# Hash attention with a maxout FFN on one Trainium2 core: who writes the hash rows, casts V and normalises

## The chip, the cores and the metric

The kernel runs on one core of a Trainium2 chip. The metric is device time in microseconds (us) of one launch, the median of three runs. PE is TensorE, DVE is VectorE, ACT is ScalarE, POOL is GpSimd, and SP is SyncE, which here only issues DMAs.

## What is computed

Attention over 4 batches, 8 heads, 768 positions, 64 dimensions per head, with a mask from a random-projection hash, followed by a feed-forward layer with a maximum of three products:

```
q_bits = (q @ proj > 0)              # 6 bits for each position
k_bits = (k @ proj > 0)
mask   = q_bucket == k_bucket        # the 6 bits read as a number
scores = where(mask, q @ k.T / 8, -1e9)
x      = softmax(scores) @ v         # then (batch*seq, heads*dim) = (3072, 512)
h      = max(x @ w1, x @ w2, x @ w3) # 512 -> 768
out    = h @ w_out                   # 768 -> 512
```

## The kernel before, in words

**Operands.** Heads go in pairs (b, pr): four pairs for each of four batches. For q and k of a pair, `split_h` (lines 139 to 146) makes a float16 high part and `split_r` (148 to 153, always DVE) the float16 remainder; both lie side by side in one tile, 128 values for a position. They are transposed into `T` (dimension by position): in batches 0 and 1 by PE (`pe_T`) with a DVE copy back (`evac_T`), in batches 2 and 3 by a transposing DMA on the SP queue (`xbar`, line 156). After the transpose the rows 0 to 63 of `T` hold the high part, the others the remainder.

**Hash rows.** `hash_mm` (172) projects `T` on PE, `hash_cmp` (183) turns the signs into +0.5 or -0.5 on DVE, and the six bits, scaled, are written into rows 64 to 69 of `T`. A score is then one matmul over 70 rows: keys of the same bucket get a fixed large bonus, which the exponential takes off again, so that others vanish. For the very first pair `hash_head` (208) writes these rows with DVE, one head at a time. For all other pairs, `hash_pair` (192) does both heads at once and scales the bits in place, and `hash_rows` (199) copies them with eight small DMAs of 4.5 KB on the SP queue (line 205).

**Units.** The work is 192 score units: a unit is two matmuls (`score`, line 244) into a PSUM tile and one exponential of 128x768 on ACT (line 253). Six units make a block, which is one half of the queries of one pair. `attend` (258) follows two units behind (LAG is 2) and accumulates into `av`, a PSUM pool with one buffer. When a block is complete, `norm` (278) adds a small term from the mean of V, takes the reciprocal (both DVE) and multiplies (POOL, line 290, but DVE for the last pair of a batch). `x_T` transposes the result on PE, with a DVE copy. `vcast` (218) casts V to float16 on POOL.

**FFN.** When a batch's half is complete, 18 first-layer atoms (four matmuls each, then an ACT copy for w1 and a DVE maximum for w2 and w3, lines 319 and 321) and three second-layer atoms (six matmuls, line 326) are put in a list. All share `mm_ps`, a PSUM pool with three buffers, with the transposes and hash products.

**Order.** The order is written out by hand: the loop over steps u (446) issues `score(u)`, `attend(u-2)`, then what `at(u, ...)` has listed, then FFN atoms as a credit allows, then what `at_end(u, ...)` has listed. Credit begins at step 41 and grows each step by `rate`, which spreads the FFN over the steps that are left. Each engine, and the SP queue, works through its own instructions in this order. `front` (387) prepares the pairs of batches 0 and 1 over some steps, `prep` (423) those of batches 2 and 3, and `tail` (402) places the hash. The hash of pair 0 of batch 2 comes at step 64, then at steps 75, 86, 97, 112, 123, 134 and 145. The loads of a pair (`load_pair`) stand eight steps ahead of its splits in the same SP queue; the first loads of batch 1 stand at step 25, behind the hash rows of batch 0 at steps 6, 15 and 22.

Of the kernel before, what the change touches and what calls it, by code (L numbers as in the profile page):

```python
# [10 lines left out]
FP16 = mybir.dt.float16  # L11
AluOp = mybir.AluOpType
# [4 lines left out]
def kernel(  # L17
# [12 lines left out]
    nc = tc.nc  # L30
    B, H, S, D = q.shape
    NBITS = proj.shape[1]
    P = 128
    NCH = S // P
# [4 lines left out]
    NP = H // 2  # L39
    HQ = S // 2  # L40
    CH = NCH // 2
# [14 lines left out]
    small = ctx.enter_context(tc.tile_pool(name="small", bufs=4))  # L56
    xp = ctx.enter_context(tc.tile_pool(name="xp", bufs=3))
    hp = ctx.enter_context(tc.tile_pool(name="hp", bufs=12))
    op = ctx.enter_context(tc.tile_pool(name="op", bufs=4))
# [38 lines left out]
    vones = []  # L98
    for i in range(2):
        t = konst.tile([P, H, NCH, D + 2], FP16, name=f"vone{i}", tag=f"vone{i}")  # L100
# [11 lines left out]
    def make_p(i):  # L112

        if i == 0:
            nc.vector.tensor_copy(ph[:], p32[:])
            nc.vector.tensor_tensor(out=pr32[:], in0=p32[:], in1=ph[:], op=AluOp.subtract)
        for o in (0, D):
            for l, src in ((PA, ph), (PB, pr32)):
                nc.vector.tensor_scalar(out=l[i][o : o + D, NBITS * i : NBITS * (i + 1)], in0=src[:],
                                        scalar1=1024.0, scalar2=None, op0=AluOp.mult)  # L120
# [10 lines left out]
    T = {}  # L131
# [7 lines left out]
    def split_h(n, b, pr, eng, heads=(0, 2)):  # L139
        a = slice(heads[0] * NCH, heads[1] * NCH)  # L140
        x32 = raws[n, b, pr][:].rearrange("p h (c d) -> p (h c) d", d=D)[:, a, :]
        o = S16[n, b, pr][:, a, 0:D]
        if eng is nc.scalar:
            nc.scalar.activation(o, x32, ActFn.Copy, scale=QS)  # L144
        else:
            eng.tensor_scalar(out=o, in0=x32, scalar1=QS, scalar2=None, op0=AluOp.mult)

    def split_r(n, b, pr, heads=(0, 2)):
        a = slice(heads[0] * NCH, heads[1] * NCH)
        x32 = raws[n, b, pr][:].rearrange("p h (c d) -> p (h c) d", d=D)[:, a, :]  # L150
        s = S16[n, b, pr]
        nc.vector.scalar_tensor_tensor(out=s[:, a, D : 2 * D], in0=x32, scalar=QS,  # L152
                                       in1=s[:, a, 0:D], op0=AluOp.mult, op1=AluOp.subtract)

    def xbar(n, b, pr):
        nc.sync.dma_start_transpose(T[n, b, pr][:], S16[n, b, pr][:].rearrange("p a d -> p (a d)"))
# [15 lines left out]
    def hash_mm(sets):  # L172

        hps = mm_ps.tile([P, 512], FP32, tag="mm", name="hps")
        ws = [(i, l[i]) for l in (PA, PB) for i in range(len(sets))]
        for m, (i, w) in enumerate(ws):
            for g, (t, hh, half) in enumerate(sets[i]):
                a = hh * NCH + half * CH
                nc.tensor.matmul(hps[32 * g : 32 * (g + 1), 0:HQ], w[:], t[:, a : a + CH, :],  # L179
                                 start=m == 0, stop=m == len(ws) - 1)  # L180
        return hps

    def hash_cmp(out, hps):
        nc.vector.tensor_scalar(out=out, in0=hps[:, 0:HQ], scalar1=0.0, scalar2=0.5,  # L184
                                op0=AluOp.is_gt, op1=AluOp.subtract)

    def hash_row(dst, src):
        nc.vector.tensor_scalar(out=dst, in0=src, scalar1=2 * BIT, scalar2=None, op0=AluOp.mult)

    hbs = {}  # L190

    def hash_pair(b, pr):
        hb = small.tile([P, HQ], FP16, tag="hb", name="hb")
        hbs[b, pr] = hb
        g = [(T[n, b, pr], hh) for hh in range(2) for n in "qk"]
        hash_cmp(hb[:], hash_mm([[(t, hh, half) for t, hh in g] for half in range(2)]))
        hash_row(hb[:], hb[:])

    def hash_rows(b, pr):
        hb = hbs.pop((b, pr))  # L200
        for g, (n, hh) in enumerate((("q", 0), ("k", 0), ("q", 1), ("k", 1))):
            for half in range(2):
                a = hh * NCH + half * CH
                o = 32 * g + NBITS * half
                nc.sync.dma_start(T[n, b, pr][D : D + NBITS, a : a + CH, :].rearrange("p a t -> p (a t)"),
                                  hb[o : o + NBITS, :])

    def hash_head(b, pr, hh):

        tq, tk = T["q", b, pr], T["k", b, pr]  # L210
        hb = small.tile([P, HQ], FP16, tag="hb", name="hb")
        hash_cmp(hb[:], hash_mm([[(tk, hh, 0), (tq, hh, 0), (tk, hh, 1), (tq, hh, 1)]]))
        for g, (t, half) in enumerate(((tk, 0), (tq, 0), (tk, 1), (tq, 1))):
            a = hh * NCH + half * CH
            hash_row(t[D : D + NBITS, a : a + CH, :].rearrange("p a t -> p (a t)"),
                     hb[32 * g : 32 * g + NBITS, :])

    def vcast(b, pr):
        v32 = raws.pop(("v", b, pr))[:].rearrange("p h (c d) -> p h c d", d=D)
        nc.gpsimd.tensor_copy(vones[b % 2][:, 2 * pr : 2 * pr + 2, :, 0:D], v32)  # L220

    mvs = {}

# [54 lines left out]
    def norm(b, hf, pr):  # L278
        av = avs.pop((b, hf, pr))[:, 0 : 2 * CH * W].rearrange("p (h c w) -> p h c w", h=2, c=CH)
        xn = xp.tile([P, CH, P], FP16, tag="xn", name="xn")  # L280
        xns[b, hf, pr] = xn
        xv = xn[:].rearrange("p c (h d) -> p h c d", h=2)
        rr = small.tile([P, 2, CH, 1], FP32, tag="rr", name="rr")
        t = small.tile([P, 2, CH, W], FP32, tag="t", name="t")
        nc.vector.tensor_tensor(out=t[:, :, :, 0 : D + 1], in0=av[:, :, :, 0 : D + 1],  # L285
                                in1=mvs[b, pr][:].unsqueeze(2).to_broadcast([P, 2, CH, D + 1]),
                                op=AluOp.add)
        nc.vector.reciprocal(rr[:], t[:, :, :, D : D + 1])  # L288
        eng = nc.vector if pr == NP - 1 else nc.gpsimd
        eng.tensor_tensor(out=xv, in0=t[:, :, :, 0:D], in1=rr[:].to_broadcast([P, 2, CH, D]),  # L290
                          op=AluOp.mult)

    def x_T(b, hf, pr):
        if (b, hf) not in xTs:
# [51 lines left out]
    todo = {}  # L346
    todo_end = {}

    def at(step, fn, pe=0.0):
        todo.setdefault(step, []).append((pe, fn))  # L350

    def at_end(step, fn):
        todo_end.setdefault(step, []).append(fn)
# [13 lines left out]
    split_h("k", 0, 0, nc.scalar, (1, 2))  # L367
    split_r("q", 0, 0, (1, 2))
    hash_head(0, 0, 0)
    make_p(1)  # L370
    vcast(0, 0)

    def first_b():
        split_r("k", 0, 0, (1, 2))
        pq = pe_T("q", 0, 0, 1)
        pk = pe_T("k", 0, 0, 1)
        evac_T(pq, "q", 0, 0, 1, nc.vector)
        evac_T(pk, "k", 0, 0, 1, nc.vector)

    at(0, first_b)  # L380
    at(1, lambda: hash_head(0, 0, 1))

    def load_pair(b, pr, eng):
        for n in "qkv":
            load(n, b, pr, eng)

    def front(b, pr, s):

        at(s, lambda: operands(b, pr))
        at_end(s, lambda: split_h("q", b, pr, nc.vector))  # L390
        at_end(s, lambda: split_h("k", b, pr, nc.vector if b == 0 else nc.scalar))
        at_end(s, lambda: split_r("q", b, pr))
        at_end(s + 1, lambda: split_r("k", b, pr))

        def tr(n, hh):
            evac_T(pe_T(n, b, pr, hh), n, b, pr, hh, nc.vector)

        for i, (n, hh) in enumerate((("q", 0), ("q", 1), ("k", 0), ("k", 1))):
            at(s + 2 + i // (2 if b == 0 else 1), lambda n=n, hh=hh: tr(n, hh), 0.34)
        tail(b, pr, s + (4 if b == 0 else 7))  # L400

    def tail(b, pr, s):
        at(s, lambda: hash_pair(b, pr), 0.67)
        at(s, lambda: hash_rows(b, pr))

    at(0, lambda: vcast(0, 1))
    at(0, lambda: load_pair(0, 2, nc.sync))
    front(0, 1, 2)
    at(2, lambda: meanv(0, 0), 0.34)
    at(3, lambda: load_pair(0, 3, nc.sync))  # L410
# [12 lines left out]
    def prep(b, pr, s):  # L423
        at(s, lambda: operands(b, pr))
        at_end(s, lambda: split_h("q", b, pr, nc.vector))
        at_end(s + 1, lambda: split_h("k", b, pr, nc.scalar))
        at_end(s + 1, lambda: split_r("q", b, pr))
        at_end(s + 1, lambda: xbar("q", b, pr))
        at_end(s + 3, lambda: split_r("k", b, pr))
        at_end(s + 3, lambda: xbar("k", b, pr))  # L430
        tail(b, pr, s + 12)

    for b in range(1, B):
        for pr in range(NP):
            s = 33 + 7 * pr if b == 1 else 2 * (b - 1) * NUG + 4 + 11 * pr
# [4 lines left out]

    N = len(units)
    begin = 6 * NUP + 5
    rate = (7 * 24 * 0.64 + sum(c for st, l in todo.items() if begin <= st < N for c, _ in l)
            + 0.2 * 28) / (N - begin)
    credit = 0.0
    for u in range(N + LAG + 4):
# [51 lines left out]
```

The softmax here doesn't subtract the row's maximum and nothing guards it: scores larger than these inputs give would overflow.

## Time and profile before

Median 319.71 us of three runs (318.12 to 321.54). The profiled execution spans 314.9 us.

| engine | busy us | share | instructions |
|---|---|---|---|
| PE | 279.7 | 89% | 2896 |
| ACT | 202.7 | 64% | 265 |
| DVE | 178.7 | 57% | 375 |
| POOL | 41.3 | 13% | 53 |

Where PE is not busy, by stretches of the timeline:

| us | steps | PE busy of it | granted PE clock |
|---|---|---|---|
| 24 to 32 | 8 to 13 | 4.11 of 8 | 0.89 |
| 32 to 40 | 13 to 18 | 7.81 of 8 | 0.68 |
| 56 to 64 | 35 to 41 | 6.14 of 8 | 1.00 |
| 72 to 80 | 47 to 51 | 6.38 of 8 | 1.00 |
| 88 to 96 | 56 to 59 | 5.47 of 8 | 0.79 |
| 120 to 128 | 75 to 77 | 4.82 of 8 | 0.65 |
| 192 to 200 | 122 to 126 | 6.03 of 8 | 1.00 |
| 208 to 216 | 132 to 136 | 5.71 of 8 | 1.00 |
| 288 to 296 | 189 to end | 5.77 of 8 | 1.00 |

A busy PE is not a PE at its peak: at a granted clock of half speed the same matmuls take longer and count as busy. The profile's chain of waits is followed back from the last instruction; a wait for several things is put down to the one that came last. "issue" is time in which an engine waited for nothing that the profile shows.

### The profile page before, as it was taken

What the parts mean: (1) busy time and instruction counts of PE and PEld (TensorE: products, weight loads), DVE (VectorE), ACT (ScalarE), POOL (GpSimd) and SP (SyncE); (2) the same over time, 40 slices, a digit from 0 to 9 for tenths busy, and PEclk for the clock granted to TensorE, in tenths of its full rate; (3) what the DMA queues carried; (4) which work ended last, traced back from release to release, by engine and by line L of the source; (5) the groups of instructions that cost most, each with busy time, mean ns of one, the idle gap of its engine ahead of it and who ended that gap; (6) DMA issues with size and microseconds to landing.
All of it is one profiled execution on the core that took longest, in us unless ns stands there. A gap on an engine that the chain in (4) does not pass through costs nothing.

```text
span 314.9 us, 7282 instructions
## 1 busy us (share of the span) xinstructions
PE 279.7 (89%) x2896; PEld 180.2 (57%) x2896; DVE 178.7 (57%) x375; ACT 202.7 (64%) x265; POOL 41.3 (13%) x53
## 2 busy tenths in 40 slices
PE   2895998798969994999999997979999999999794
PEld 1463765565647562565666664636666665665451
DVE  5766582797876652556476564736463454443552
ACT  3346479877736773676777776675767777777220
POOL 0304512120041101101102121120101110111000
PEclk9999699999989997799999999999999999999999
DMA  7905993918136058190938427092802002001002
GB/s 202 371 30 72 143 180 84 352 46 285 41 52 186 10 89 266 31 227 6 235 122 217 136 55 205 14 271 76 104 4 103 2 1 98 5 3 67 35 0 100
DMA packets 47138, 35.63 MB, mean 113 GB/s; under 512 B 27184, under 2 KB 44032, under 8 KB 47104
## 3 DMA queue, kind: packets, MB, share of 16 engines
q1 hardware_dynamic: 43072, 32.02, 36.7%
q0 software_dynamic: 3952, 3.15, 7.0%
q8 instruction: 22, 0.36, 0.4%
q14 instruction: 12, 0.10, 0.1%
q10 hardware_dynamic: 80, 0.00, 0.0%
HBM read 25.17 MB, written 6.29 MB: 100 GB/s over the span
## 4 chain that ended last, share of the span: by engine, by line
PE 74%; DMA 12%; DVE 8%; ACT 3%; issue 2%; SPq 0%; ACTq 0%; DVEq 0%
PE ps L314 27%; PE sc L249 17%; PE po L326 9%; PE av L269 9%; DMA kT<-ks 7%; PE hps L179 5%; PE tps L162 4%; ACT AT L253 3%; DMA k<-in_k_dram 2%; PE xps L300 2%; DVE ks L152 2%; DMA kT<-hb 1%; PE svp L228 1%; DMA q<-in_q_dram 1%; DVE hb L184 1%
## 5 line engine op out<-in xcount | busy, mean ns | idle before, releaser
L253 ACT ACTIVATE AT<-sc,bias_t 128x768 f16<-128x768 f32 x192 | 169.7, 901 | 73.4 <-PE sc L249 72.5
L314 PE MATMUL ps<-xT,w_sb 128*128 128x384 f16 x576 | 112.8, 330 | 4.2 <-DVE mv L231 4.2
L249 PE MATMUL sc<-qT,kT 70*128 70x384 f16 x384 | 98.6, 339 | 7.0 <-DMA kT<-hb 3.3
L269 PEld LDWEIGHTS <-AT 128*128 128x128 f16 x1152 | 62.4, 99 | 28.9 <-issue 4.6
L321 DVE TENSOR_TENSOR ht<-ht,ps 128x384 f16<-128x384 f16 x96 | 52.9, 551 | 45.3 <-PE ps L314 40.8
L269 PE MATMUL av<-vone,AT 128*128 128x65 f16 x1152 | 68.4, 196 | 1.4 <-ACT AT L253 0.7
L314 PEld LDWEIGHTS <-w_sb 128*128 128x128 f16 x576 | 51.3, 98 | 31.7 <-issue 6.4
L249 PEld LDWEIGHTS <-kT 70*128 70x128 f16 x384 | 34.1, 100 | 28.3 <-issue 7.9
L290 POOL TENSOR_TENSOR xn<-t,rr 128x384 f16<-128x384 f32 x24 | 20.6, 859 | 210.4 <-DVE rr L288 116.5
L319 ACT CAST ht<-ps 128x384 f16<-128x384 f32 x48 | 22.8, 475 | 21.4 <-PE ps L314 21.3
L326 PE MATMUL po<-wout_sb,ht 128*128 128x512 f16 x144 | 34.7, 379 | 0.0
L285 DVE TENSOR_TENSOR t<-av,mv 128x390 f32<-128x390 f32 x32 | 18.0, 562 | 12.3 <-PE av L269 12.2
L332 DVE COPY osb<-po 128x512 f32<-128x512 f32 x16 | 11.1, 692 | 20.6 <-PE po L326 20.6
L184 DVE TENSOR_SCALAR hb<-hps 128x384 f16<-128x384 f32 x17 | 9.5, 557 | 20.9 <-PE hps L179 20.8
L326 PEld LDWEIGHTS <-ht 128*128 128x128 f16 x144 | 13.0, 97 | 12.6
L220 POOL CAST vone<-v 128x768 f16<-128x768 f32 x16 | 15.0, 942 | 35.6 <-DMA v<-in_v_dram 35.5
L179 PE MATMUL hps<-kT,PA 128*32 128x384 f16 x64 | 9.6, 363 | 9.7 <-DMA kT<-ks 8.8
L301 DVE COPY xT<-xps 128x384 f16<-128x384 f16 x32 | 11.3, 354 | 12.0 <-PE xps L300 11.6
L152 DVE SCALAR_TENSOR_TENSOR ks<-k,ks 128x768 f16<-128x768 f32 (+1 forms) x17 | 17.0, 1003 | 0.3 <-ACT ks L144 0.2
L152 DVE SCALAR_TENSOR_TENSOR qs<-q,qs 128x768 f16<-128x768 f32 (+1 forms) x17 | 15.4, 906 | 0.2
L162 PE MATMUL tps<-iden,qs 128*128 128x128 f16 x96 | 9.4, 254 | 6.8 <-DVE qs L152 6.8
L144 ACT ACTIVATE ks<-k 128x768 f16<-128x768 f32 (+1 forms) x14 | 11.1, 796 | 4.0 <-DMA k<-in_k_dram 4.0
(43 smaller groups left out, 160.3 us busy)
## 6 DMA issues: line engine op xcount, KB each, us to landing
v<-in_v_dram SPq DMA_DIRECT2D x16, 384.0 KB
out_dram<-osb SPq DMA_DIRECT2D x24, 256.0 KB
q<-in_q_dram SPq DMA_DIRECT2D x15, 384.0 KB
k<-in_k_dram SPq DMA_DIRECT2D x15, 384.0 KB
w_sb<-in_moe_w_dram POOLq DMA_DIRECT2D x6, 384.0 KB, 6.9
qT<-hb SPq DMA_DIRECT2D x60, 4.5 KB
kT<-hb SPq DMA_DIRECT2D x60, 4.5 KB
wout_sb<-in_moe_w_out_dram POOLq DMA_DIRECT2D x1, 768.0 KB, 13.3
```

The source lines that it names most:

```text
L152: nc.vector.scalar_tensor_tensor(out=s[:, a, D : 2 * D], in0=x32, scalar=QS, in1=s[:, a, 0:D], op0=AluOp.mult, op1=AluOp.subtract)
L162: nc.tensor.transpose(p16[:, c * P : (c + 1) * P], S16[n, b, pr][:, hh * NCH + c, :], iden[:])
L179: nc.tensor.matmul(hps[32 * g : 32 * (g + 1), 0:HQ], w[:], t[:, a : a + CH, :], start=m == 0, stop=m == len(ws) - 1)
L249: nc.tensor.matmul(sc[:, i, 0:HQ], kT[0:KR, hh * NCH + 2 * j + i, :], qT[0:KR, hh * NCH + hf * CH : hh * NCH + (hf + 1) * CH, :], start=Tr ...
L253: nc.scalar.activation(AT[:], sc[:, :, 0:HQ], ActFn.Exp, bias=bias_t[:], scale=EXP_SCALE)
L269: nc.tensor.matmul(av[:, o : o + D + 1], AT[:, i, c * P : (c + 1) * P], vones[b % 2][:, 2 * pr + hh, 2 * j + i, 0 : D + 1], start=first, s ...
L285: nc.vector.tensor_tensor(out=t[:, :, :, 0 : D + 1], in0=av[:, :, :, 0 : D + 1], in1=mvs[b, pr][:].unsqueeze(2).to_broadcast([P, 2, CH, D ...
L290: eng.tensor_tensor(out=xv, in0=t[:, :, :, 0:D], in1=rr[:].to_broadcast([P, 2, CH, D]), op=AluOp.mult)
L314: nc.tensor.matmul(ps[:, 0:HQ], w_sb[i][:, jc, fb * P : (fb + 1) * P], xT[:, jc, :], start=jc == 0, stop=jc == NJ - 1)
L319: nc.scalar.copy(ht[:], ps[:, 0:HQ])
L321: nc.vector.tensor_tensor(out=hts[fb][:], in0=hts[fb][:], in1=ps[:, 0:HQ], op=AluOp.max)
L326: nc.tensor.matmul(ps[:], hts[fb][:, c * P : (c + 1) * P], wout_sb[:, fb, :], start=fb == 0, stop=fb == NF - 1)
```

## The change

Five edits. Hash rows are written by DVE, not by DMA, in all batches but batch 1, and the hash of a pair is done in two halves: one of the queries' and keys' halves each. `vcast` goes from POOL to ACT from batch 1 on. The multiplication in `norm` is always on DVE, and the high part of k, which ACT made from batch 1 on, is made by DVE. In the first pair, the remainder of head 1's k is made ahead of the first score unit, and the transposes of head 1 come one step later, as does its hash. The planned FFN rate is a little lower, by 3.2 us of matmul time over the whole loop. It is meant to take the small DMAs out of the SP queue and the work off POOL, and to leave FFN atoms for the end.

```diff
+    def hash_half(b, pr, half):
+        if half == 0:
+            hbs[b, pr] = small.tile([P, S], FP16, tag="hb2", name="hb2")
+        g = [(T[n, b, pr], hh, half) for hh in range(2) for n in "qk"]
+        hash_cmp(hbs[b, pr][:, half * HQ : (half + 1) * HQ], hash_mm([g]))
+
+    def hash_head_rows(b, pr, hh):
+        for i, n in enumerate("qk"):
+            dst = T[n, b, pr][D : D + NBITS, hh * NCH : (hh + 1) * NCH, :].rearrange("p a t -> p (a t)")
+            o = 32 * (2 * hh + i)
+            hash_row(dst, hbs[b, pr][o : o + NBITS, :])
...
     def vcast(b, pr):
-        nc.gpsimd.tensor_copy(vones[b % 2][:, 2 * pr : 2 * pr + 2, :, 0:D], v32)
+        o = vones[b % 2][:, 2 * pr : 2 * pr + 2, :, 0:D]
+        if b == 0:
+            nc.gpsimd.tensor_copy(o, v32)
+        else:
+            nc.scalar.copy(o, v32)
...
-        eng = nc.vector if pr == NP - 1 else nc.gpsimd
-        eng.tensor_tensor(out=xv, in0=t[:, :, :, 0:D], in1=rr[:].to_broadcast([P, 2, CH, D]),
-                          op=AluOp.mult)
+        nc.vector.tensor_tensor(out=xv, in0=t[:, :, :, 0:D], in1=rr[:].to_broadcast([P, 2, CH, D]),
+                                op=AluOp.mult)
...
-    make_p(1)
+    split_r("k", 0, 0, (1, 2))
...
-        split_r("k", 0, 0, (1, 2))
...
-    at(0, first_b)
-    at(1, lambda: hash_head(0, 0, 1))
+    at(1, first_b)
+    at(2, lambda: hash_head(0, 0, 1))
...
-        at_end(s, lambda: split_h("k", b, pr, nc.vector if b == 0 else nc.scalar))
+        at_end(s, lambda: split_h("k", b, pr, nc.vector))
...
     def tail(b, pr, s):
-        at(s, lambda: hash_pair(b, pr), 0.67)
-        at(s, lambda: hash_rows(b, pr))
+        if b == 1:
+            at(s, lambda: hash_pair(b, pr), 0.67)
+            at(s, lambda: hash_rows(b, pr))
+        else:
+            at(s, lambda: hash_half(b, pr, 0), 0.34)
+            at(s + (b > 0), lambda: hash_half(b, pr, 1), 0.34)
+            for hh in range(2):
+                at_end(s + (b > 0) * (1 + hh), lambda hh=hh: hash_head_rows(b, pr, hh))
...
+    at(2, lambda: make_p(1))
...
-        at_end(s + 1, lambda: split_h("k", b, pr, nc.scalar))
+        at_end(s + 2, lambda: split_h("k", b, pr, nc.vector))
...
-    rate = (7 * 24 * 0.64 + sum(c for st, l in todo.items() if begin <= st < N for c, _ in l)
+    rate = (7 * 24 * 0.64 - 3.2 + sum(c for st, l in todo.items() if begin <= st < N for c, _ in l)
             + 0.2 * 28) / (N - begin)
```

## The prediction, on record before the changed kernel ran

> **What bounds the kernel now.** I read the busy shares first, then the waits by total, the chain of waits in order of time, and the SP queue's timeline where the chain turns to a DMA. The busy shares:
>
> ```profile
> PE 279.7 (89%) x2896; PEld 180.2 (57%) x2896; DVE 178.7 (57%) x375; ACT 202.7 (64%) x265; POOL 41.3 (13%) x53
> PEclk9999699999989997799999999999999999999999
> ```
>
> PE is the bound, but not evenly: its 35 us of idle time lie in a few places, and three dips of the clock follow three of them. The table of waits says for what PE stops, and why the SP queue is late:
>
> ```profile
> PE hps L179 <- DMA kT<-ks: 8.8, 4, 4.3
> PE ps L314 <- DVE mv L231: 4.2, 2, 2.5
> PE sc L249 <- DMA kT<-hb: 3.3, 2, 2.1
> ...
> SPq L205 <- DVE hb L188: 65.3, 13, 14.6
> ```
>
> The first and third are DMAs of the SP queue. The chain at these places:
>
> ```profile
> 27.12 4.69 DMA kT<-hb
> 52.90 3.70 DMA k<-in_k_dram
> 117.81 5.33 DMA kT<-ks
> ```
>
> The SP queue's timeline ahead of the third:
>
> ```profile
> 101.12 1.49 SPq L205 DMA_DIRECT2D qT<-hb  x2
> ...
> 111.59 1.43 SPq L205 DMA_DIRECT2D kT<-hb  x2
> 113.10 1.46 SPq L156 DMA_TRANSPOSE qT<-qs  x1
> ...
> 117.81 2.76 SPq L156 DMA_TRANSPOSE kT<-ks  x1
> ```
>
> Sixteen hash-row DMAs of two pairs take (113.02 - 101.12) / 16 = 0.74 us of the queue each. The transposes of the next pair queue behind them, and at step 75 PE stands 4.30 us in the hash product. So the transfers are late because they are issued late. The other PE wait, at 89 us, is DVE's:
>
> ```profile
> 88.80 2.94 DVE L152 SCALAR_TENSOR_TENSOR ks<-k,ks 128x768 f16<-128x768 f32 x2
> 89.37 3.05 POOL L220 CAST vone<-v 128x768 f16<-128x768 f32 x2
> ```
>
> Two operations that alone take 0.95 us (DVE) and 0.83 us (POOL) take about 1.5 us each while they overlap.
>
> [...]
>
> **Prices.** DVE multiplication of `norm`: 0.56 us (line 290 on DVE), for 0.83 on POOL. High part of k on DVE: 0.55 (line 146, median), for 0.84 on ACT. V cast on ACT: not in the trace; the same shape and types on ACT take 0.84 (line 144), so ACT gains and loses 0.84 for each of 12 pairs: zero. Comparison: 0.56 (line 184); one more for a pair. A hash row of 6x768 float16: the trace has 6x384 at 0.25. Bounds 0.25 and 0.50 (doubled). A float32 split goes from 0.36 to 0.55 as 384 elements become 768, so 0.19; half of it in 16 bits gives 0.35, which I take. The in-place scaling (0.26) goes. A pair that changes its hash thus costs DVE 0.56 + 4 x 0.35 - 0.26 = 1.7 us, and frees 8 x 0.74 = 5.9 us of the SP queue.
>
> **Part by part, as four stretches.**
>
> *Start (steps 0 to 6).* The edit to the first pair lets the second exponential start about 1 us sooner, but score 3 waits for head 1's rows in both orders, and the small `make_p(1)` (4 x 0.16) now stands ahead of the next splits on DVE. Zero, give or take 0.5.
>
> *A. Steps 6 to 36, 21.1 to 58.4 us: 37.3 us.* The waits for hash rows (2.05 at step 11, 1.26 at step 13) go, as the rows take DVE until about step 8 and are read at step 12. With them goes the clock dip: 8 x 0.11 + 8 x 0.32 = 3.4 us. The 1.84 us at step 35 wait for loads that stood in the queue behind three pairs' hash rows (issued at 52.4 us for a place at step 25); with no rows there, they are issued far ahead. PE's work here is 30.7 busy less 3.4 = 27.3 us; the 30 exponentials are 30 x 0.85 = 25.5. DVE's is about 21.7 busy by the table of windows + 3 x 1.7 + 5 x 0.56 + 0.55 = 30.2 us: DVE becomes the bound of this stretch. With a gap or two, 31.6. **-5.7 us** (-3 to -9).
>
> *B. Steps 40 to 63, 61.6 to 101.3 us: 39.7 us.* Batch 1 is prepared here with PE transposes; its hash rows stay with the DMAs. PE idles 4.8 us and loses 8 x 0.21 = 1.7 to the clock, so its work is 33.2. DVE is busy 31.4; it loses 1.2 of stretching by POOL and gains 4 x 0.55 + 3 x 0.56 = 3.9: 34.1. Two engines at about the same level overlap imperfectly; before, that gave some 2 us of waits (step 50: 1.62) at lower DVE load. I take 38.2. **-1.5** (-4 to +2).
>
> *C. Steps 63 to 147, 101.3 to 231 us.* The waits for the transposes go: 4.30 + 0.20 + 1.97 + 2.29 = 8.8, and the dip after step 75: 8 x 0.35 + 8 x 0.08 = 3.4. The q transposes come 6 us sooner, which covers each wait. The V cast on ACT could make the exponentials queue behind a late V; its load stands 12 steps ahead, some 16 us, and the queue is free, so zero. Against it: DVE goes from 72 busy to 72 + 8 x (1.7 + 0.55) + 10 x 0.56 = 96 us, in about 118. The additions come bunched: in three steps of some 1.3 us DVE gets 0.56 + 0.95, then 0.56 + 0.55 + 0.70, then 0.95 + 0.70, beside some 0.4 a step for the FFN, so about 6.2 us in 4. A norm (0.56 + 0.19 + 0.56) falls into or right after this in most pairs. Behind it PE stands when a fourth product needs one of the three PSUM buffers, or the next block needs `av`. I walked one pair (step 112) along PE's timeline: DVE ends some 2 us after PE would need the buffer when a norm follows directly, less than 1 otherwise. In the six pairs with splits of the next one beside them, some 1 us each: 6 us. **12.2 - 6 = -6.2** (0 to -12).
>
> *D. The end.* PE idles 2.23 us after the last unit while the last norm and transpose are awaited. With 3.2 us of FFN atoms left over, these fill it: **-2.2** (-1.5 to -2.3). From step 147 to 190 nothing but the norms changes on DVE, which is half idle.
>
> Sum: -5.7 - 1.5 - 6.2 - 2.2 = -15.6; 319.7 - 15.6 = **304 us**.
>
> **Rivals.** *R1, DVE takes PE's place in C and B:* stalls of 2.3 us in all eight pairs, 18 us, and B at +2: -5.7 + 2 + 5.8 - 2.2, about 320, no change. For it: the wait for `mv` in the table, 4.2 us at 57% of DVE. Against: in steady state DVE bursts of 3 us (182.4 to 185) passed without idle PE. *R2, slower:* stalls of 3 us in the eight pairs, 24, A gives only 3, B +3, and the stalls drop the clock once (3.4): -3 + 3 + 11.8 + 3.4 - 2.2 = +13, 333 us. Against it: 13 us of DVE work for 15 of PE in each pair of C. *R3, the bursts are absorbed:* no stalls in C and 4 us in B: -5.7 - 4 - 12.2 - 2.2 = -24, 296 us. For it: PE's order puts score, attend and hash between atoms, and a third of the atoms go to ACT.
>
> **How the numbers follow.** Forecast (299 to 311) 0.60, R3 (below 299) 0.18, R1 (311 to 323) 0.15, R2 0.07. The range leaves out R2, the better part of R1 and the far end of R3: 294 to 313. Faster by over 1% (below 316.5): forecast, R3 and a third of R1, 0.83; within 1%: 0.07; slower: 0.10.
>
> **What would show it.** Right: no PE wait for kT<-ks or kT<-hb from steps 6 to 36 and 64 to 147; no clock dip at 30 and 122 us; hash rows of about 0.35 us on DVE; POOL nearly idle after 60 us; new PE waits for DVE (`av`, PSUM buffers) of some 6 us in C; DVE near 225 us busy. Wrong: PE waits for DVE above 15 us in all; hash rows of 0.5 us or more; exponentials that wait behind V casts; the transposes still late after batch 1's own hash rows.

## The result, and the profile after

The changed kernel takes 308.09 us (median of four runs, 305.96 to 309.71), the kernel before 318.91 (four runs, 317.24 to 321.54). The ratio is 0.9649, with a 95% interval of 0.9558 to 0.9741. The forecast was 304 us with a range of 294 to 313: the direction and the range hold, but of the 15.6 us of gain that were added up, 10.8 came. The experiments below ran on three chips, four on each in the order of the text; the kernel before has medians of 317.92, 318.87 and 317.61 us on them. A ratio leaves out runs that count as slow, which on the third chip leaves three of seven runs of the kernel before, 312.84 to 315.92 us, and makes the ratios there some 0.7% higher than the medians would.

The page of the changed kernel, busy shares and granted clock:

```profile
PE 276.1 (90%) x2896; PEld 176.6 (58%) x2896; DVE 212.0 (69%) x455; ACT 200.6 (66%) x265; POOL 9.3 (3%) x17
PEclk9969979999997999999999999999999999999998
```

DVE gained 33 us of work and POOL lost 32. The dip at 120 us is gone, and from 96 us on there is none before the last 3 us. The dip at 17 to 24 us is no loss against the kernel before, whose score matmuls took as long there, 0.83 to 0.85 us a pair, without a record of it: its clock record begins at 23.4 us, that of the changed kernel at 13.7. The same pair, in the kernel before and, ahead of the dip, in the changed kernel:

```profile
15.69 0.83 PE L249 MATMUL sc<-qT,kT 70*128 70x384 f16 x2
```

```profile
14.21 0.50 PE L265 MATMUL sc<-qT,kT 70*128 70x384 f16 x2 [0.27 <-DVE qT L188]
```

In the recorded dips, at a granted clock of 0.50, such a pair takes 0.81 to 0.85 us as well. The waits of PE, by total:

```profile
PE tps L162 <- DVE qs L152: 11.9, 7, 4.3
PE av L285 <- DVE t L301: 4.3, 4, 1.9
PE ps L329 <- DVE ht L336: 1.7, 1, 1.7
...
SPq L217 <- DVE hb L188: 35.2, 3, 30.5
```

No wait of PE for a DMA is left in the table: those for kT<-ks (8.8 us) and kT<-hb (3.3) are gone. What PE waits for now is DVE. The SP queue at the place where the transposes were late:

```profile
104.31 1.43 SPq L217 DMA_DIRECT2D qT<-hb  x2
105.79 1.43 SPq L217 DMA_DIRECT2D kT<-hb  x2
107.31 1.45 SPq L156 DMA_TRANSPOSE qT<-qs  x1
...
111.35 3.30 SPq L156 DMA_TRANSPOSE kT<-ks  x1
```

One pair's rows stand there instead of two pairs', the transposes are issued 6 us sooner, and the hash product at step 75 (119 us) does not wait.

For the rest I cut the trace at the first score matmul of steps 6, 36, 40, 63, 147 and 191, and took for each stretch its length and PE's idle time in it; "dip" is the recorded time at half clock (0.50 granted), times one half; the slow matmuls ahead of the record (to 23.4 us before, to 13.7 after) are not in it. All in us, from the profiled runs:

| stretch | before | after | difference | predicted |
|---|---|---|---|---|
| steps 0 to 6 | 12.4 (idle 1.5) | 14.4 (idle 4.4, dip 3.1) | +2.0 | 0 |
| A, 6 to 36 | 37.3 (idle 7.5, dip 3.4) | 34.7 (idle 6.4, dip 2.0) | -2.5 | -5.7 |
| 36 to 40 | 3.2 | 3.9 (idle 0.7) | +0.7 | 0 |
| B, 40 to 63 | 39.7 (idle 4.8, dip 1.7) | 39.4 (idle 4.7, dip 1.7) | -0.3 | -1.5 |
| C, 63 to 147 | 129.8 (idle 8.8, dip 3.4) | 120.1 (idle 2.5) | -9.7 | -6.2 |
| 147 to 191 | 60.3 | 59.0 | -1.3 | with the end |
| step 191 to the end | 23.5 (idle 6.2) | 25.7 (idle 4.7) | +2.2 | -2.2 |
| span | 314.9 | 306.0 | -8.9 | -15.6 |

One profiled run holds chance too: rows_only and rows_rate, below, are the same program up to step 41, and A takes 34.4 us without a dip in the one and 37.9 with 5.1 us of dips in the other.

### The profile page after: what moved, and what is told of

Read it like the earlier page. It is cut to its first block, busy times and chain, and to the rows that moved or that the text cites. A ratio compares the mean times of both kernels' runs of the same rounds, so it can differ in the third digit from the quotient of the medians.

```text
span 306.0 us, 7090 instructions
## 1 busy us (share of the span) xinstructions
PE 276.1 (90%) x2896; PEld 176.6 (58%) x2896; DVE 212.0 (69%) x455; ACT 200.6 (66%) x265; POOL 9.3 (3%) x17
## 4 chain that ended last, share of the span: by engine, by line
PE 74%; DVE 18%; ACT 3%; issue 2%; DMA 1%; SPq 0%; DVEq 0%; ACTq 0%
PE ps L329 28%; PE sc L265 16%; PE av L285 9%; PE po L341 9%; PE hps L179 4%; PE tps L162 4%; DVE qs L152 3%; ACT AT L269 2%; DVE hb L184 2%; DVE ks L146 2%; DVE ks L152 2%; PE xps L315 2%; DVE kT L188 2%; PE svp L244 1%; DVE t L301 1%
## 5 line engine op out<-in xcount | busy, mean ns | idle before, releaser
L265 PE MATMUL sc<-qT,kT 70*128 70x384 f16 x384 | 96.4, 332 | 4.2 <-ACT AT L269 1.6
L285 PEld LDWEIGHTS <-AT 128*128 128x128 f16 x1152 | 61.3, 98 | 31.1 <-issue 6.9
L336 DVE TENSOR_TENSOR ht<-ht,ps 128x384 f16<-128x384 f16 x96 | 52.9, 552 | 34.4 <-PE ps L329 31.6
L285 PE MATMUL av<-vone,AT 128*128 128x65 f16 x1152 | 67.1, 193 | 4.4 <-DVE t L301 4.3
L184 DVE TENSOR_SCALAR hb<-hps 128x384 f16<-128x384 f32 x28 | 15.2, 553 | 8.7 <-PE hps L179 8.6
L162 PE MATMUL tps<-iden,qs 128*128 128x128 f16 x96 | 9.7, 259 | 12.7 <-DVE qs L152 11.9
L305 DVE TENSOR_TENSOR xn<-t,rr 128x384 f16<-128x384 f32 x32 | 17.9, 558 | 1.1
L152 DVE SCALAR_TENSOR_TENSOR qs<-q,qs 128x768 f16<-128x768 f32 (+1 forms) x17 | 16.5, 972 | 0.1
L162 PEld LDWEIGHTS <-qs 128*128 128x128 f16 x96 | 7.4, 116 | 14.7 <-DVE qs L152 13.3
L316 DVE COPY xT<-xps 128x384 f16<-128x384 f16 x32 | 11.3, 353 | 6.2 <-PE xps L315 5.9
L152 DVE SCALAR_TENSOR_TENSOR ks<-k,ks 128x768 f16<-128x768 f32 (+1 forms) x17 | 15.3, 906 | 0.3
L179 PE MATMUL hps<-kT,PA 128*32 128x384 f16 x64 | 11.1, 343 | 1.0 <-DVE kT L170 0.9
L170 DVE COPY kT<-tps 128x768 f16<-128x768 f16 x16 | 8.6, 553 | 4.3 <-PE tps L162 4.2
```

The costliest lines, as they stand in the source:

```text
L162: nc.tensor.transpose(p16[:, c * P : (c + 1) * P], S16[n, b, pr][:, hh * NCH + c, :], iden[:])
L265: nc.tensor.matmul(sc[:, i, 0:HQ], kT[0:KR, hh * NCH + 2 * j + i, :], qT[0:KR, hh * NCH + hf * CH : hh * NCH + (hf + 1) * CH, :], start=Tr ...
L285: nc.tensor.matmul(av[:, o : o + D + 1], AT[:, i, c * P : (c + 1) * P], vones[b % 2][:, 2 * pr + hh, 2 * j + i, 0 : D + 1], start=first, s ...
L336: nc.vector.tensor_tensor(out=hts[fb][:], in0=hts[fb][:], in1=ps[:, 0:HQ], op=AluOp.max)
```

## Experiments

**Theory:** the gain is the SP queue's, which DVE's row writes set free; the missing part of it went to the start (weight loads that POOL now issues early) and to the work moved onto DVE and ACT. **Rival:** the gain is POOL's relief, since a split on DVE took some 1.5 us for 0.95 beside POOL's V casts; or DVE's total load is the bound wherever it is put.

### Which edit brings the gain

The rows alone, on the kernel before:

```diff
     def tail(b, pr, s):
-        at(s, lambda: hash_pair(b, pr), 0.67)
-        at(s, lambda: hash_rows(b, pr))
+        if b == 1:
...
+        else:
+            at(s, lambda: hash_half(b, pr, 0), 0.34)
...
```

> The kernel before with one edit alone: the hash rows of batches 0, 2 and 3 written by DVE in two halves, as in the changed kernel. Theory (the gain is the SP queue's, 5.9 us of it for each pair): this edit alone gives most of the gain, 309 to 312 us for some 319 of the kernel before, the waits for kT<-ks after step 64 are gone, and steps 63 to 147 take 8 to 11 us less. Rival (the gain is the work taken off POOL[...]): less than a third of the gain, 316 us or more.

Measured (rows_only): 307.28 us (303.60 to 308.85), ratio 0.9645 (0.9545 to 0.9745), below the expected 309. Stretch C takes 119.8 us for 129.8, A 34.4 for 37.3.

The engine moves alone, on the kernel before:

```diff
-        nc.gpsimd.tensor_copy(vones[b % 2][:, 2 * pr : 2 * pr + 2, :, 0:D], v32)
+        if b == 0:
+            nc.gpsimd.tensor_copy(o, v32)
+        else:
+            nc.scalar.copy(o, v32)
...
-        eng = nc.vector if pr == NP - 1 else nc.gpsimd
...
-        at_end(s + 1, lambda: split_h("k", b, pr, nc.scalar))
+        at_end(s + 2, lambda: split_h("k", b, pr, nc.vector))
```

> The kernel before with the engine moves alone: V cast on ACT from batch 1 on, all norm multiplications and the high part of k on DVE; hash rows stay DMAs. Theory (the gain is the SP queue's): the waits for kT<-hb and kT<-ks stay, time 317 to 322 us, at or above the kernel before. Rival (POOL relief): 312 us or less, and steps 40 to 63 at least 3 us shorter.

Measured (relief_only): 322.88 us (321.88 to 324.92), ratio 1.0177 (1.0087 to 1.0267): slower. B takes 43.5 us for 39.7, all but 0.3 us of it in longer dips. Its table of waits still has both DMA waits:

```profile
PE hps L179 <- DMA kT<-ks: 10.2, 4, 4.0
...
PE sc L253 <- DMA kT<-hb: 4.3, 2, 3.7
```

So the row edit alone has the whole gain of the changed kernel, and the engine moves by themselves lose 1.8%. POOL's relief is not the cause of the gain. The five edits together bring no more than one of them.

### The start: early work on POOL

In the changed kernel POOL, which no longer waits for norms, runs straight into the weight loads and the V cast of the fourth pair, which stands between them. The timelines of POOL, of DVE and of PE at 15 to 20 us:

```profile
14.87 3.12 POOL L128 DMA_DIRECT2D w_sb<-in_moe_w_dram  x4
17.95 0.87 POOL L234 CAST vone<-v 128x768 f16<-128x768 f32 x1
18.71 1.52 POOL L128 DMA_DIRECT2D w_sb<-in_moe_w_dram  x2
```

```profile
17.56 2.09 DVE L152 SCALAR_TENSOR_TENSOR qs<-q,qs 128x768 f16<-128x768 f32 x1
```

```profile
19.70 1.46 PE L162 MATMUL tps<-iden,qs 128*128 128x128 f16 x12 [4.09 <-DVE qs L152]
```

The split of q takes 2.09 us there, for 0.95 in the kernel before (16.60 us). In the kernel before, POOL issued the loads from 26.2 us on, behind the first norm. To put that gate back with next to no other work on POOL (the V cast then stands behind the gate as well):

```diff
+    gate = konst.tile([P, 1], FP16, name="gate")
+    at(7, lambda: nc.gpsimd.tensor_copy(gate[:], xns[0, 0, 0][:, 0, 0:1]))
     for i in range(3):
         at(7 + i, lambda i=i: load_w(i, 0))
```

> The changed kernel, with a one-element POOL copy of the first block's result ahead of the weight loads, so that these can't be issued ahead of step 7, as in the kernel before. Theory (POOL, freed of the norms, issues the weight loads at 15 to 21 us, [...]): that split is back at about 0.95 us, PE's wait of 4.1 us at step 4 falls below 2, and step 6 starts 1.5 to 2.5 us sooner; total 1 to 2 us less, some 306.5 us. Rival (the wait at step 4 is made by the new order of the first pair's work on DVE): the wait stays at 3 us or more, total as the changed kernel, 308.

Measured (w_gate): 306.50 us (305.27 to 308.32), ratio 0.9663 (0.9591 to 0.9736); that overlaps the changed kernel's interval, so the total does not show it. The trace does. DVE and PE in this run:

```profile
17.32 0.95 DVE L152 SCALAR_TENSOR_TENSOR qs<-q,qs 128x768 f16<-128x768 f32 x1
```

```profile
18.32 1.46 PE L162 MATMUL tps<-iden,qs 128*128 128x128 f16 x12 [2.01 <-DVE qs L152]
```

The split is back at 0.95 us, and PE's wait is halved; steps 0 to 6 take 12.7 us for 14.4. The other half of the wait is not the early POOL work's. And the collision is moved rather than removed: at 31.55 us the q split of the next pair now takes 1.56 us beside the same cast and loads, and A takes 36.8 us for 34.7, though part of that (0.7) is a longer dip. The wait also varies: rate_undo and no_swap run the same program as the changed kernel up to here, and PE waits 2.90 and 3.88 us in them. In rate_undo no q split is slowed (0.951 us in the mean of 15), while the k splits take 1.07 us more in all than in the changed kernel (1.024 for 0.953 in the mean of 15). The timelines of rows_rate_norm, below, show such a pair: its q split falls ahead of the V cast, beside weight loads alone, and takes 0.94 us; its k split, which meets the cast, takes 1.99. A split was thus doubled where it met the V cast, not beside the loads alone, on which the theory had put it.

### The lower FFN rate

```diff
-    rate = (7 * 24 * 0.64 - 3.2 + sum(c for st, l in todo.items() if begin <= st < N for c, _ in l)
+    rate = (7 * 24 * 0.64 + sum(c for st, l in todo.items() if begin <= st < N for c, _ in l)
```

> The changed kernel with the FFN rate of the kernel before (without the 3.2 us). Theory (leftover FFN atoms fill PE's wait for the last norm): PE idles some 2 us again after the last unit, total 310 us. Rival (the lower rate only moves work from the loop to the end): 308 us, unchanged.

Measured (rate_undo): 314.01 us (312.02 to 315.44), ratio 0.9891 (0.9818 to 0.9964): without this edit two thirds of the changed kernel's gain are lost. PE's timeline after the last unit in this run, and in the changed kernel:

```profile
288.19 0.36 PE L285 MATMUL av<-vone,AT 128*128 128x65 f16 x6 [0.69 <-ACT AT L269]
290.02 0.50 PE L315 MATMUL xps<-iden,xn 128*128 128x128 f16 x3 [1.48 <-DVE xn L305]
```

```profile
283.74 1.46 PE L341 MATMUL po<-wout_sb,ht 128*128 128x512 f16 x6
285.38 0.34 PE L315 MATMUL xps<-iden,xn 128*128 128x128 f16 x3 [0.18 <-DVE xn L305]
```

The waits of 0.69 and 1.48 us are filled, as was forecast for 2.2 us. The edit brought more than that, 5.9 us between the medians, and the stretches say where: B is 2.5 us shorter in the changed kernel than in this run (1.7 of it a dip), C 1.9 (1.0 of it idle time, the rest work that moved to the end), and a dip that costs 1.7 us after the last unit is gone. That fewer atoms in a step let fewer of DVE's bursts reach PE would explain the idle time; no run shows it alone. On the rows-only kernel the same edit gave:

> The kernel before with the hash rows on DVE in batches 0, 2 and 3 and the lower FFN rate, nothing else. Theory (these two edits are all of the gain, the engine moves cost more than they bring): 303 to 305.5 us, below the changed kernel's 308; PE does not idle after the last unit. Rival (the engine moves pay for themselves once the SP queue is free): 308 us or more.

Measured (rows_rate): 302.79 us (301.99 to 305.25), ratio 0.9559 (0.9482 to 0.9637), 4.5 us below the rows alone; the intervals overlap. Two of the five edits are faster than all five: 302.8 for 308.1 in the medians, with no run in common, though the intervals of the two ratios touch.

### The other edits, one at a time on top of these two

All norm multiplications on DVE:

```diff
-        eng = nc.vector if pr == NP - 1 else nc.gpsimd
-        eng.tensor_tensor(out=xv, in0=t[:, :, :, 0:D], in1=rr[:].to_broadcast([P, 2, CH, D]),
+        nc.vector.tensor_tensor(out=xv, in0=t[:, :, :, 0:D], in1=rr[:].to_broadcast([P, 2, CH, D]),
```

> Rows on DVE and the lower rate, with all norm multiplications on DVE as well. Theory (POOL, without norms, issues the weight loads into the first pairs' splits, and DVE has 13 us more to do): 2 to 4 us more than rows and rate alone, 306 to 308, with the wait at step 4 longer. Rival [...]: no more than rows and rate alone.

Measured (rows_rate_norm): 302.83 us (301.11 to 303.85), ratio 0.9542 (0.9467 to 0.9617): no difference, against my theory. Here too the weight loads are issued from 14.9 us on, but PE's wait at step 4 is only 1.12 us. The timelines of DVE and POOL show why: the q split stands earlier, and the one that meets the V cast is k's, which PE needs a step later. PE's score pairs also still take 0.83 to 0.85 us here up to 22.2 us, where the changed kernel's took 0.50 at 14.2, and PE comes to step 4 later.

```profile
16.88 0.94 DVE L152 SCALAR_TENSOR_TENSOR qs<-q,qs 128x768 f16<-128x768 f32 x1
17.74 1.99 DVE L152 SCALAR_TENSOR_TENSOR ks<-k,ks 128x768 f16<-128x768 f32 x1
```

```profile
14.93 3.15 POOL L128 DMA_DIRECT2D w_sb<-in_moe_w_dram  x4
18.05 0.86 POOL L232 CAST vone<-v 128x768 f16<-128x768 f32 x1
```

The first pair's new order puts `make_p(1)` ahead of the q split on DVE, which moves that split later, toward the cast. That order alone:

```diff
-    at(0, first_b)
-    at(1, lambda: hash_head(0, 0, 1))
+    at(1, first_b)
+    at(2, lambda: hash_head(0, 0, 1))
...
+    at(2, lambda: make_p(1))
```

> Rows on DVE and the lower rate, with the new order of the first pair (head 1 behind two score units). Theory (score 3 waits for head 1's rows in both orders): within 1 us of rows and rate alone. Rival (the new order puts more DVE work ahead of the second pair's splits and PE waits at step 4): 1.5 us or more above it.

Measured (rows_rate_first): 300.73 us (299.51 to 301.17), ratio 0.9468 (0.9395 to 0.9541): all four runs below all four of rows and rate alone, which neither theory nor rival said. It is the fastest kernel of this study. Steps 0 to 6 are no shorter (12.6 us for 12.0, and PE's wait at step 4 is 1.6 for 0.9). The difference is in the clock: its profiled run (mean granted clock 0.998) has no dip before the last stretch, where rows and rate alone (0.977) has 5.1 us of dips in A and 1.7 in B.

```profile
PEclk9999999999999999999999999999999999999999
```

PE's waits for DVE are no shorter (some 18 us in the table of waits, for 16), so what the traces show of the gain is clock, not waits. That the order is its cause is not shown: rows_rate_norm, with the old order, has no such dip either, and k_dve below, with the new one, has one of 3.4 us in B.

The swap, V cast to ACT and high part of k to DVE:

```diff
-        nc.gpsimd.tensor_copy(vones[b % 2][:, 2 * pr : 2 * pr + 2, :, 0:D], v32)
...
+            nc.scalar.copy(o, v32)
...
-        at_end(s + 1, lambda: split_h("k", b, pr, nc.scalar))
+        at_end(s + 2, lambda: split_h("k", b, pr, nc.vector))
```

> Rows on DVE and the lower rate, with the V cast on ACT and the high part of k on DVE from batch 1 on; norms as in the kernel before. Theory (the high part of k, 0.55 us on DVE ahead of the splits, delays PE's transposes in batch 1, steps 40 to 63): 1 to 3 us more than rows and rate alone. Rival (the overlap of POOL's V cast with DVE, 1.5 us for 0.95, is worth more than that): 1 us less or better.

Measured (rows_rate_swap): 305.59 us (303.43 to 306.47), ratio 0.9624 (0.9546 to 0.9703), 2.8 us more; the intervals overlap. C takes 120.4 us for 118.5. One cost is the V cast itself, which delays an exponential at step 39, where the exponentials are the bound:

```profile
61.70 0.48 PE L265 MATMUL sc<-qT,kT 70*128 70x384 f16 x2 [0.69 <-ACT AT L269]
```

The same taken from the other side, the changed kernel with only the swap undone:

```diff
...
-            nc.scalar.copy(o, v32)
+        nc.gpsimd.tensor_copy(vones[b % 2][:, 2 * pr : 2 * pr + 2, :, 0:D], v32)
...
-        at_end(s + 2, lambda: split_h("k", b, pr, nc.vector))
+        at_end(s + 1, lambda: split_h("k", b, pr, nc.scalar))
```

> The changed kernel with the swap between ACT and POOL/DVE undone: V cast on POOL and the high part of k on ACT from batch 1 on, as in the kernel before; rows, norms, first pair and rate as changed. Theory (the swap alone costs some 3 us, and the early weight loads 1.6): 304 to 305.5 us. Rival (the swap is only harmless noise and the four other edits together cost what the changed kernel lacks): 307 us or more.

Measured (no_swap): 304.98 us (302.78 to 305.56), ratio 0.9674 (0.9562 to 0.9787); all its runs are below the 305.96 to 309.71 of the changed kernel, by 3.1 us in the median. The two were timed on different occasions, and the ratios don't separate them; with the 2.8 us above, some 3 us is likely rather than shown. Steps 36 to 40 are back at 3.2 us and B is at 36.5 for 39.4 (1.7 of it a dip). PE's wait at step 4 stays, 3.88 us: that part is not the swap's. One half of the swap, the high part of k on DVE, on top of the fastest kernel:

```diff
-        at_end(s, lambda: split_h("k", b, pr, nc.vector if b == 0 else nc.scalar))
+        at_end(s, lambda: split_h("k", b, pr, nc.vector))
...
-        at_end(s + 1, lambda: split_h("k", b, pr, nc.scalar))
+        at_end(s + 2, lambda: split_h("k", b, pr, nc.vector))
```

> Rows on DVE, lower rate and the first pair's new order (300.7 us), with the high part of k on DVE from batch 1 on, and the V cast left on POOL: one half of the swap. Theory (the cost of the swap is the high part of k ahead of other work on DVE): 302.5 to 304 us. Rival (the cost is the V cast on ACT, which delays exponentials): 301 us or less.

Measured (k_dve): 307.78 us (305.58 to 308.66), ratio 0.9768 (0.9677 to 0.9860): 7 us more, clear of the fastest kernel's interval, and more than I expected. B takes 41.4 us for 37.2 (idle 5.1 for 3.7, and a dip of 3.4 for none), C 120.1 for 118.5. In PE's timeline the same waits stand longer, ahead of the transposes at steps 42, 49 and 56 and of an FFN atom, here first in this kernel, then in the fastest:

```profile
64.31 0.51 PE L162 MATMUL tps<-iden,qs 128*128 128x128 f16 x6 [0.62 <-DVE qs L152]
74.75 0.51 PE L162 MATMUL tps<-iden,qs 128*128 128x128 f16 x6 [0.72 <-DVE qs L152]
...
85.86 0.51 PE L162 MATMUL tps<-iden,qs 128*128 128x128 f16 x6 [0.90 <-DVE qs L152]
87.47 0.81 PE L326 MATMUL ps<-xT,w_sb 128*128 128x384 f16 x4 [1.10 <-DVE ht L333]
```

```profile
63.73 0.51 PE L162 MATMUL tps<-iden,qs 128*128 128x128 f16 x6 [0.28 <-DVE qs L152]
73.83 0.51 PE L162 MATMUL tps<-iden,qs 128*128 128x128 f16 x6 [0.38 <-DVE qs L152]
...
84.59 0.51 PE L162 MATMUL tps<-iden,qs 128*128 128x128 f16 x6 [0.56 <-DVE qs L152]
85.73 0.81 PE L326 MATMUL ps<-xT,w_sb 128*128 128x384 f16 x4 [0.63 <-DVE ht L333]
```

Each wait for the q remainder grows by 0.34 us, with 0.55 us more ahead of it on DVE. Of the 6.3 us between the two profiled runs, 3.4 are the dip and some 3 idle time. The high part of k is the expensive half. Whether the V cast on ACT, for all its 0.7 us at step 39, gives some of it back in the full swap stays open; it was not run alone.

### Batch 1, and the order in batch 0

Why the rows of batch 1 stay with the DMAs:

```diff
-        if b == 1:
+        if False:
             at(s, lambda: hash_pair(b, pr), 0.67)
```

> Rows on DVE, lower rate and the first pair's new order (300.7 us), with the hash rows of batch 1 on DVE as well. Theory (steps 40 to 63 are near DVE's limit, and no transpose waits for the SP queue any more): 1 to 4 us more, most of it in steps 40 to 66. Rival (the SP queue still holds something back in batch 1): 1 us less or better.

Measured (best_rows_all): 310.02 us (308.32 to 311.49), ratio 0.9848 (0.9749 to 0.9948): 9.3 us more than the fastest kernel, and far more than expected. B takes 46.1 us for 37.2, with 7.9 idle and 5.1 in dips. (A, where the two programs are the same, takes 2.6 us more through dips.) In B alone the exception for batch 1 is worth nearly as much as the row edit brought in C. C is 0.8 us shorter there (0.6 us idle for 1.5), but the wait that is gone, 0.90 us at step 68, is one for DVE's norm; that the SP queue still held something back is not shown.

The rows of batch 0 behind the norm, not ahead of it:

```diff
-                at_end(s + (b > 0) * (1 + hh), lambda hh=hh: hash_head_rows(b, pr, hh))
+                at_end(s + 1 + hh, lambda hh=hh: hash_head_rows(b, pr, hh))
```

> Rows on DVE, lower rate and the first pair's new order (300.7 us), with the rows of batch 0 written one and two steps later, so that the norm of the block goes ahead of them on DVE. Theory (PE's 1.93 us at step 8 is the norm behind four row writes): that wait falls below 0.7, steps 6 to 36 take 1 to 1.5 us less, some 299.5 us. Rival (DVE's total is the bound of the stretch): the waits move to later steps, total within 0.5 us.

Measured (best_rows_late): 300.86 us (300.45 to 301.23), ratio 0.9559 (0.9494 to 0.9623): no difference to the 300.73. PE's wait at step 8 falls from 1.93 us to 0.33, as the theory said, and A is 34.3 us in both, as the rival said. Idle time in A falls by 1.6 us, and a dip takes 1.7. In place of the wait removed, the clock was lower (0.994 in the mean of the profiled run, for 0.998).

## Why the prediction was right, and where it was wrong

**Right: the bound of C.** The transposes were late because hash-row DMAs held the SP queue. The row edit alone takes 10.0 us off C; the 3.4 us dip is gone in every kernel that has it, and so are the 8.8 us of waits (0.4 us is left in no_swap). The row writes cost what was worked out, 0.353 us for 0.35:

```profile
L188 DVE TENSOR_SCALAR kT<-hb 6x768 f16<-6x768 f16 x22 | 7.8, 353 | 0.4
```

The halving for 16 bits in that price was an estimate, which this case bears out: 384 more elements of a float16 row cost 0.10 us (0.25 to 0.353), 384 more of the split from float32 0.19 (0.36 to 0.55).

**Mis-sized in C, to the good:** the term "six pairs, some 1 us each: 6 us". DVE was busy 90 us there for the 96 that were worked out, but PE idled only 2.5 us, at steps 68, 80 and 116, each time for a norm; the 3.5 us below the 6 are the difference between -6.2 and -9.7. The lower rate, which the prediction had put wholly at the end, shortens C by 1.2 to 1.9 us, in part by work that moves to the end.

**Wrong: "Start: zero, give or take 0.5".** It was +2.0: 2.9 us more idle time, 0.9 less busy. The step looked at what the first pair's edit does on PE and did not ask what POOL does once the norms no longer hold it. Half of PE's 4.1 us at step 4 goes when that work, the weight loads and a V cast, is held back (w_gate). It hurts with the first pair's new order beside it: over all runs, steps 0 to 6 take 13.0 to 14.6 us with both, 12.6 to 12.7 with the new order alone, 12.2 to 12.5 with the early POOL work alone, and 12.0 to 12.4 with neither (10.5 in rows_only).

**Wrong: A, "-5.7, DVE becomes the bound, with a gap or two 31.6".** DVE's load was, if anything, too high (27.8 busy, 30.2 worked out), yet the stretch took 34.7. Of the 3.4 us dip, which was to go with the waits ahead of it (an estimate, from the three dips that follow idle time in the kernel before), 2.0 stayed, and PE's work before was 29.7 us busy, not 30.7. DVE's work there is not back to back: PE waits for DVE at steps 8, 14 and 20 (1.94, 1.12 and 1.05 us), and DVE for PE in between. Adding up an engine's work gave a floor, and it was taken for the time. Moving one of these waits away gave nothing (best_rows_late).

**Wrong: the V cast, "so zero", and B, "-1.5".** "ACT gains and loses 0.84" is true of its sum (0.824 measured), but steps 36 to 40 are bound by the exponentials, and a cast there costs 0.7. In B, which came out at -0.3, the 0.55 us of the high part of k, counted in DVE's total, stands ahead of the splits that PE waits for; the swap seems to cost about 3 us in the changed kernel. In the profiled runs 6.7 us are missing: 3.2 in A, 2.0 at the start, 1.9 in steps 36 to 63, while C and the end together miss the forecast by 0.4 the other way.

**Too small: D, -2.2.** The idle time at the end falls by 2.0 us, as described, but the edit is worth 4.5 to 5.9 us in the medians; the rest lies in B, in C and in the clock.

**Rivals.** R1, DVE in PE's place, is what happens in B when more is put on DVE (k_dve, best_rows_all), not in the changed kernel as a whole. In C the stalls, 2.5 us, lie between R3's none and the forecast's 6. The sign "no clock dip at 30 us" held only in part, as a dip came at 41 us. DVE was busy 212 us in all, for "near 225", where the prediction's own terms add up to some 217. One of the other signs named for a wrong prediction was badly chosen: PE waits for DVE for more than 15 us in all, some 22 in the table of waits, but the kernel before had some 16 of them already.

## What to carry to other kernels

Before moving work off an engine, ask what that engine's queue was holding back: the norms on POOL were the gate of the weight loads and of a V cast. Price moved work by what stands right behind it in the new queue, not by its share of the engine's total: the high part of k, 0.55 us for each of 12 pairs but in front of splits, cost 7 us, about half of it clock, while 15.5 us of row writes in batches 0, 2 and 3 fitted in. And when several edits come together, run each alone: here one edit carried the gain, another added to it, and a third seems to have taken some 3 us of it away again.

## What was not expected of the hardware

Half-speed dips (a granted clock of 0.50) set kernels of nearly the same waits apart. In rows and rate alone, A has 6.4 us idle and 5.1 in dips, with the first pair's new order 7.4 idle and none. All its four runs have a mean granted clock of 0.992 or more; those of rows and rate alone 0.977 to 0.993. In the kernel before and the changed kernel the dips before the last 3 us last 3.4 or 6.8 us each; what sets their start and length no run here shows. A difference of some 3 us in such a kernel can be clock alone: A takes 34.4 us without a dip in rows_only and 37.9 with 5.1 us of dips in rows_rate, the same program up to there. And the clock record does not show all of it: ahead of its first entry, or with no dip in it, a pair of score matmuls took 0.80 to 0.85 us in the kernel before (8.7 to 21.1 us), the changed kernel (11.3), rows_rate_norm (14.6 to 21.4), rows_rate_first (19.6) and best_rows_late (21.7), for 0.49 later.

The remainder of q, 0.95 us alone, took 0.94 beside weight loads that POOL issues (rows_rate_norm, 16.9 us). With a V cast of POOL beside it as well, it took 1.56 (w_gate, 31.6 us) and 2.09 (changed kernel, 17.6 us), and that of k 1.99 (rows_rate_norm, 17.7 us). The high part is slower beside the loads: 0.82 us at 27.4 and at 28.2 us in the kernel before, for 0.55.
